# Scores of the unsplit tiles on 64 rows per head, with two PSUM banks of their own

## The chip, the core and the metric

The kernel runs on one core of a Trainium2 chip. The metric is the time of one execution on the device in microseconds (us). A core has a matrix engine (TensorE, PE in the profile, its weight loads shown apart as PEld), VectorE (DVE), ScalarE (ACT), GpSimd (POOL) and SyncE (SP), which here issues nearly all DMAs. Each engine takes its instructions in order; between engines they wait for semaphores. Matmuls write to PSUM, an accumulator memory of eight banks with 512 float32 per partition each; VectorE and ScalarE read it from there.

## What is computed

Attention over 512 local and 32 global positions in 8 batches of 8 heads of width 64, with a band of 32 positions to either side for the local ones, and then an expert layer over all 4608 tokens. Everything is float32. Cut to what matters:

```python
s_l = concat([scale * q_l @ k_g.T, where(|i - j| <= 32, scale * q_l @ k_l.T, -1e9)])
out_l = softmax(s_l) @ concat([v_g, v_l])
out_g = softmax(scale * q_g @ concat([k_g, k_l]).T) @ concat([v_g, v_l])
x = concat([out_g, out_l]) as [4608 tokens, 512]
h = max(x @ w1, x @ w2, x @ w3)
return h @ w_out
```

## The kernel before

**Tiles.** A pair of heads `p` has four tiles of 128 queries (`t` = 0 to 3), 128 tiles in all. A tile sees a window of 192 keys (`t` = 0, 3) or 224 (`t` = 1, 2), since the band reaches no further and the 32 global keys are put among the others. For each tile `scores` (L314) makes one score block per head in PSUM, VectorE adds the mask and takes the row minimum (L342), ScalarE takes the exponential (L344), and the row is normalised. `trans` (L355) transposes the probabilities on TensorE into the tile `T`; a copy `pt` of it feeds `pv` (L391), the product with `v`. `transg`, `glob` and, for the first four pairs, `late` do the same for the global queries. `layer1` (L441) and `layer2` (L462) are the expert layer.

**Split and unsplit tiles.** From tile 28 on, float32 operands are split into two parts that a faster form of the matmul takes (`split_q`, `split_k`, L339). The first 28 tiles (`NATK`) use plain float32 (L335). There the keys of both heads lie in one tile, head 0 on partitions 0 to 63 and head 1 on 64 to 127, and the host sends `q` as 128 x 256: for each head 128 columns with the other head's 64 rows set to zero. So one matmul over all 128 rows gives one head's scores. In the profile such a matmul has two records. `pv` of the first 26 tiles (L401) writes head 0 to output partitions 0 to 63 and head 1 to 64 to 127, on 64 columns of the array each (128*64 in the profile).

**PSUM.** Of the eight banks, three belong to the expert layer (`pm`), two to the pool `psS` (tiles named S, two buffers), one to `T`, and two to the pool `psO` (a tile named O of two banks, one buffer). S is used by `scores`, `glob`, `transg` and `late`; O by `pv` and by the last step of `late` (L519). Accesses of one tile in the same bank are kept in order across engines, whichever columns they touch.

**Order.** A loop over the tiles in the order `SEQ` (L209) puts, for tile i: `transg`, `trans` of tile i + 1, a few layer-1 matmuls of an earlier batch (`fill`), `scores` of tile i + 3, `pv` of tile i, a step of the global queries, loads and, for 24 steps, a piece of the weights, which arrive as float64 and are converted on ScalarE, VectorE and GpSimd (L175 to L181). A scheduler then reorders the instructions of each engine within what the data allow. Tiles 0 to 15 (`EARLY`) come in an order that does half a sequence of four pairs at a time, and their probabilities stay in SBUF (`early`); from tile 16 on they go through a DMA into `prob`, from which they are transposed.

Of the kernel before, what the change touches and what calls it, by code (L numbers as in the profile page):

```python
# [9 lines left out]
F32 = mybir.dt.float32  # L10
# [8 lines left out]
B, H, SL, SG, D = 8, 8, 512, 32, 64  # L19
DM, DF = 512, 768  # L20
NP = H // 2
# [4 lines left out]
NATK = range(0, 28)  # L26
# [24 lines left out]
def f32(ap):  # L51
    return ap.bitcast(F32)


def body(ctx, tc, kin, qin, vin, min_, win, out):
    nc = tc.nc
    act, dve, pool, pe = nc.scalar, nc.vector, nc.gpsimd, nc.tensor

    const = ctx.enter_context(tc.tile_pool(name="const", bufs=1))
    att = ctx.enter_context(tc.tile_pool(name="att", bufs=2))  # L60
# [3 lines left out]
    psS = ctx.enter_context(tc.tile_pool(name="psS", bufs=2, space=PSUM))  # L64
    psT = ctx.enter_context(tc.tile_pool(name="psT", bufs=1, space=PSUM))
    psO = ctx.enter_context(tc.tile_pool(name="psO", bufs=1, space=PSUM))
# [15 lines left out]
    def spend(es, ns):  # L82
        for e in es:
            load[e] += ns
# [69 lines left out]
    turned = psT.tile([128, 512], F32, name="T")  # L154
    dve.memset(turned, 0.0)

    spare = [moe.tile([128, 2, 512], I32, name="spare", tag=f"h{f}") for f in (4, 5)]
    loaded, marks = [0], {}

# [47 lines left out]
    NAT = 26  # L207
    EARLY = 16
    SEQ = [4 * p + t for h in range(2) for p in range(NP) for t in (2 * h, 2 * h + 1)] + list(range(16, NS))  # L209
    kraw, kst, qraw, qs, vraw, vs, xr, sc, pg, pts = [{} for _ in range(10)]  # L210
# [32 lines left out]
    def load_q(s):  # L243
        if s < NS:
            if s in NATK:
                e = s < EARLY and SEQ.index(s) % 2
                qraw[s] = att.tile([128, 256], F32, name="qn", tag="qraw" if e else "qs")
            else:
                qraw[s] = att.tile([128, 256], F32, name="qraw")
            nc.sync.dma_start(out=qraw[s], in_=qin[s])  # L250

    def split_q(s):
        if s < NS and s not in NATK:
# [60 lines left out]
    def scores(sl):  # L314
        if sl >= NS:
            return
        p, t = divmod(sl, 4)
        c0, n = WIN[t]
        ps = psS.tile([128, 512], F32, name="S")
        if sl < EARLY:  # L320
            s = sc[sl] = early[:, SEQ.index(sl) % 4]
        else:
            s = att.tile([128, 2, 224], F32, name="s")
            sc[sl] = prob[sl % 2]
        nm = small.tile([128, 2], F32, name="nm")
        z = small.tile([128, 2], F32, name="z")
        ph = [ps[:, 0:224], ps[:, 224:448]]
        if sl < EARLY:
            keys, c0 = khalf[p][0], c0 - khalf[p][1]
        elif sl in NATK:  # L330
            keys = kraw[p]
        for j in range(2):
            if sl in NATK:

                pe.matmul(ph[j][:, 0:n], lhsT=qraw[sl][:, 128 * j:128 * j + 128], rhs=keys[:, c0:c0 + n],  # L335
                          start=True, stop=True)
                continue
            for a in range(2):
                pe.matmul(ph[j][:, 0:n], lhsT=qs[sl][:, a, 128 * j:128 * j + 128],  # L339
                          rhs=kst[p][:, j, c0:c0 + n], start=(a == 0), stop=(a == 1))  # L340
        for j in range(2):
            dve.tensor_tensor_reduce(out=s[:, j, 0:n], in0=ph[j][:, 0:n], in1=mask[:, (1, 0, 1, 0)[t], 32 * (t == 0):32 * (t == 0) + n],  # L342
                                     scale=-0.125, scalar=3.0e38, op0=ALU.add, op1=ALU.min, accum_out=nm[:, j:j + 1])
            act.activation(out=s[:, j, 0:n], in_=s[:, j, 0:n], func=AF.Exp, bias=nm[:, j:j + 1], scale=-1.0,  # L344
                           accum_out=z[:, j:j + 1])
        for j in range(2):
            dve.tensor_scalar(out=z[:, j:j + 1], in0=z[:, j:j + 1], scalar1=1e-9, scalar2=None, op0=ALU.add)  # L347
            dve.reciprocal(out=z[:, j:j + 1], in_=z[:, j:j + 1])
            times(s[:, j, 0:n], s[:, j, 0:n], z[:, j:j + 1])
        if sl >= EARLY:  # L350
            nc.sync.dma_start(out=f32(sc[sl])[:, :, 0:n], in_=s[:, :, 0:n])
        spend("d", 2 * (n * 1.04 + 75) + 150)
        spend("a", 2 * (n * 0.833 + 278))
# [37 lines left out]
    def pv(sl):  # L391
        p, t = divmod(sl, 4)
        pt = pts.pop(sl)
        o = psO.tile([128, 2, 512], F32, name="O")
        if t == 0:
            xr[p] = xp.tile([128, 4, 160], F32, name="xr")
        if sl < NAT:

            for c, j in ((0, 0), (0, 1), (1, 0), (1, 1)):
                n = 160 if sl >= EARLY and c < GCH[t][2] else 128  # L400
                pe.matmul(o[64 * j:64 * j + 64, 0, 0:n], lhsT=vraw[sl][:, 2 * j + c], rhs=pt[:, j, c, 0:n], start=(c == 0), stop=(c == 1))  # L401
            n = 160 if sl >= EARLY else 128
            copy(xr[p][:, t, 0:n], o[:, 0, 0:n], True)
        else:

            for j in range(2):
                for c in range(2):
                    n = 160 if c < GCH[t][2] else 128
                    pe.matmul(o[:, j, 0:320].rearrange("p (a q) -> p a q", a=2)[:, :, 0:n],  # L409
                              lhsT=vs[sl][:, 2 * j + c].rearrange("p a d -> p (a d)"),  # L410
                              rhs=pt[:, j, c, :, 0:n], start=(c == 0), stop=(c == 1))
            lo = att.tile([64, 2, 160], F32, name="lox", bufs=1)
            copy(lo, o[64:128, :, 0:160], True)
            spend("d", 460 + 2 * 320)
            dve.tensor_tensor(out=lo, in0=o[0:64, :, 160:320], in1=lo, op=ALU.add)
            for j in range(2):
                dve.tensor_tensor(out=xr[p][64 * j:64 * j + 64, t], in0=o[0:64, j, 0:160], in1=lo[:, j], op=ALU.add)  # L417
        if t == 3 and sl >= EARLY:
            dve.tensor_reduce(out=xg[:, p % NP, p // NP], in_=xr[p][:, :, 128:160].rearrange("p t g -> p g t"),
                              axis=AX.X, op=ALU.add)  # L420
# [75 lines left out]
    def late(p):  # L496
        k, v = side[:, 0:640], side[:, 640:1664].rearrange("p (t x) -> p t x", t=4)
        nc.sync.dma_start(out=k, in_=kin[p])
        nc.sync.dma_start(out=v, in_=vin[4 * p:4 * p + 4].rearrange("t p x -> p t x"))
        yield  # L500
        s, nm, z = side[0:64, 0:NG], small.tile([64, 2], F32, name="nmg"), small.tile([64, 2], F32, name="zg")
        for i, (c0, n) in enumerate(SEG):
            ps = psS.tile([128, 512], F32, name="S")
            pe.matmul(ps[0:64, 0:n], lhsT=k[:, KW:KW + 2 * SG], rhs=k[:, c0:c0 + n], start=True, stop=True)
            dve.tensor_tensor_reduce(out=s[:, 384 * i:384 * i + n], in0=ps[0:64, 0:n], in1=zero[0:64].to_broadcast([64, n]),
                                     scale=-0.125, scalar=3.0e38, op0=ALU.add, op1=ALU.min, accum_out=nm[:, i:i + 1])
            spend("d", n * 1.04 + 75)
        yield
        soft(s, nm, z)
        yield  # L510
        g = psS.tile([128, 512], F32, name="S")
        for x, (t, c, c0) in enumerate(PARTS):
            pe.transpose(g[:, 64 * x:64 * x + 64], side[0:64, c0:c0 + 128], one[0:64, 0:64])
        gt = att.tile([128, 6, 64], F32, name="gt", tag="lox", bufs=1)
        dve.tensor_tensor(out=gt, in0=g[:, 0:384].rearrange("p (x g) -> p x g", g=64), in1=cover.to_broadcast([128, 6, 64]), op=ALU.mult)
        o = psO.tile([128, 2, 512], F32, name="O")
        for x, (t, c, _) in enumerate(PARTS):
            for j in range(2):
                pe.matmul(o[64 * j:64 * j + 64, 0, 0:SG], lhsT=v[:, t, 64 * (2 * j + c):64 * (2 * j + c) + 64],  # L519
                          rhs=gt[:, x, SG * j:SG * j + SG], start=(x == 0), stop=(x == 5))  # L520
        copy(xg[:, p, 0], o[:, 0, 0:SG], True)
        yield
# [44 lines left out]
    for i, sl in enumerate(SEQ):  # L567
# [52 lines left out]
        elif i % 16 >= 12:  # L620
            q = b * NP + i % 16 - 12
# [9 lines left out]
def _pack(q_l, k_l, v_l, q_g, k_g, v_g):  # L631
# [8 lines left out]
    g = np.concatenate([ga, gb], axis=3).transpose(0, 1, 3, 4, 2, 5).reshape(B, NP, 128, 2 * SG)  # L640
    k = np.ascontiguousarray(np.concatenate([k, g], axis=3)).reshape(B * NP, 128, KW + 2 * SG)
    q = q_l.reshape(B, NP, 2, 4, 128, D).transpose(0, 1, 3, 5, 2, 4).reshape(B * NP * 4, D, 256)
    q2 = q.reshape(B * NP * 4, D, 2, 128)
    z = np.zeros_like(q2[:, :, 0])
    qz = np.concatenate([np.concatenate([q2[:, :, 0], z], axis=2), np.concatenate([z, q2[:, :, 1]], axis=2)], axis=1)
    q = np.concatenate([q, q], axis=1)
    q[NATK.start:NATK.stop] = qz[NATK.start:NATK.stop]
    vt = [v_l[:, :, 32 * u:32 * u + 32] for u in range(16)] + [v_g]
    zero = np.zeros_like(v_g)
    v = np.concatenate([x for r in VROWS for x in [vt[u] for u in r] + [zero] * (4 - len(r))], axis=2)  # L650
# [1 line left out]
    q, v = np.ascontiguousarray(q), np.ascontiguousarray(v)  # L652
# [34 lines left out]
```

## Time and profile before

| | us |
|---|---|
| runs of before: median of three | 828.65 |
| runs of before: lowest, highest | 827.93, 828.94 |
| the profiled execution's own time | 830.49 |
| its span, first to last instruction | 828.7 |
| TensorE busy | 803.0 |
| VectorE busy | 614.8 |
| ScalarE busy | 510.2 |
| GpSimd busy | 459.3 |

Busy times are those of the profiled execution and overlap one another. A row of the timeline gives the start in us from the span's start, the duration in us, the engine, the line of the kernel, the operation, the tile written and those read, the part of the array that a matmul uses (rows*columns), the shape and the number of records put together; in brackets stands how long the engine had been idle and what ended that. Starts of matmuls are measured and their ends are modelled, so times between starts are used.

### The profile page before, as it was taken

Reading aid. Unit: us, or ns where it says so; the run is one execution under the profiler, and the core shown is the slowest. Engines: PE = TensorE matmul, PEld = TensorE weight load, DVE = VectorE, ACT = ScalarE, POOL = GpSimd, SP = SyncE. Lnnn points to the kernel's source line nnn. Section 1 sums busy time; section 2 is a strip of 40 time slices with the busy share of each in tenths; the row PEclk is TensorE's granted clock in tenths of the full one; section 3 lists DMA queues with packets and bytes.
Section 4 is the critical chain, followed back from the end, with each engine's and each line's share of the span. In section 5 each row is a group of like instructions: output and inputs, shape, how many; then the busy total and the mean of one; then the engine's idle time right before and its main releaser. Section 6 shows DMA issues by size and latency. Waiting matters only on the chain.

```text
span 828.7 us, 16580 instructions
## 1 busy us (share of the span) xinstructions
PE 803.0 (97%) x4772; PEld 683.8 (83%) x4772; DVE 614.8 (74%) x2192; ACT 510.2 (62%) x1416; POOL 459.3 (55%) x623
## 2 busy tenths in 40 slices
PE   6788999999999999999999999999999999999997
PEld 5577888888888888888888888888888888888896
DVE  6999997878887888888887888788887888412111
ACT  5888786666666666666766667676666666311111
POOL 3223355756676667767675676866776665311211
PEclk9989999999999999999999999999999999999999
DMA  8956555533335333443335333443335332100001
GB/s 295 314 178 224 169 152 149 165 116 99 116 108 152 112 97 104 131 136 94 99 104 170 112 98 97 127 139 98 97 96 165 110 100 63 60 13 1 25 27 26
DMA packets 97466, 98.15 MB, mean 118 GB/s; under 512 B 19296, under 2 KB 85856, under 8 KB 97376
## 3 DMA queue, kind: packets, MB, share of 16 engines
q1 hardware_dynamic: 97232, 96.87, 38.0%
q8 instruction: 38, 0.62, 0.3%
q14 instruction: 52, 0.43, 0.2%
q10 hardware_dynamic: 144, 0.23, 0.1%
HBM read 60.39 MB, written 8.91 MB: 84 GB/s over the span
## 4 chain that ended last, share of the span: by engine, by line
PE 80%; DVE 5%; DMA 4%; issue 3%; ACT 3%; POOL 3%; SPq 1%; POOLq 0%; ACTq 0%; DVEq 0%
PE pm L441 45%; PE pm L462 16%; PE O L409 6%; PE S L339 5%; PE T L362 2%; PE T L363 2%; DMA prob<-s 2%; PE S L289 1%; PE S L335 1%; POOL h L103 1%; PE O L401 1%; DMA vraw<-v_in 1%; ACT s L344 1%; PE S L381 1%; DMA raw<-w_in 1%
## 5 line engine op out<-in xcount | busy, mean ns | idle before, releaser
L441 PE MATMUL pm<-xs,w 128*128 128x512 f32 (+1 forms) x2160 | 487.3, 366 | 1.3 <-ACT m L115 0.9
L441 PEld LDWEIGHTS pm<-xs,w 128*128 128x128 f32 x2160 | 354.3, 190 | 52.7 <-issue 4.2
L462 PE MATMUL pm<-w,h 128*128 128x512 f32 x612 | 157.5, 397 | 2.3 <-POOL h L103 2.1
L103 POOL TENSOR_TENSOR h<-m,h 128x512 fp32r<-128x512 f32 (+1 forms) x59 | 70.3, 1192 | 108.5 <-ACT h L115 107.9
L462 PEld LDWEIGHTS pm<-w,h 128*128 128x128 f32 x612 | 109.0, 188 | 23.0 <-POOL h L103 4.4
L450 DVE TENSOR_TENSOR m<-pm,m 128x512 f32<-128x512 f32 (+1 forms) x120 | 72.8, 607 | 66.3 <-PE pm L441 65.6
L103 POOL TENSOR_TENSOR qs<-qraw,qs 128x256 fp32r<-128x256 f32 x100 | 76.7, 767 | 70.4 <-issue 34.8
L344 ACT ACTIVATE s<-s,nm 128x192 f32<-128x192 f32 (+1 forms) x224 | 103.3, 462 | 19.6 <-DVE nm L342 14.1
L125 POOL TENSOR_SCALAR s<-s,z 128x224 f32<-128x224 f32 (+1 forms) x192 | 83.9, 444 | 36.1 <-ACT lox L115 20.4
L342 DVE CUSTOM_DVE_ANT_0 s<-S,mask 128x192 f32<-128x192 f32 (+1 forms) x224 | 74.5, 369 | 15.2 <-PE S L339 7.0
L103 DVE TENSOR_TENSOR pt<-T,pt 128x512 fp32r<-128x512 f32 x102 | 70.4, 690 | 19.4 <-ACT pt L115 18.2
L103 POOL TENSOR_TENSOR vs<-vraw,vs 128x256 fp32r<-128x256 f32 x102 | 75.6, 741 | 12.6 <-ACT vs L115 9.3
L409 PEld LDWEIGHTS O<-pt,vs 128*128 128x128 f32 x408 | 66.2, 188 | 9.9 <-issue 1.6
L409 PE MATMUL O<-pt,vs 128*128 128x320 f32 (+1 forms) x408 | 72.9, 300 | 1.4 <-DVE pt L103 1.4
L339 PEld LDWEIGHTS S<-kst,qs 128*128 128x128 f32 x400 | 59.5, 190 | 8.7 <-DVE nmg L293 0.2
L417 DVE TENSOR_TENSOR xr<-O,lox 64x160 f32<-64x160 f32 x204 | 64.4, 315 | 3.1
L103 POOL TENSOR_TENSOR kst<-kraw,kst 64x576 fp32r<-64x576 f32 x44 | 63.9, 1453 | 4.3 <-DMA prob<-s 1.0
L115 ACT CAST pt<-T 128x512 fp32r<-128x512 f32 x102 | 60.3, 591 | 9.5 <-PE T L363 7.1
L115 ACT CAST qs<-qraw 128x256 fp32r<-128x256 f32 x94 | 38.3, 407 | 44.0 <-PE S L339 28.8
L115 ACT CAST h<-m 128x512 fp32r<-128x512 f32 (+1 forms) x59 | 33.2, 562 | 51.7 <-DVE m L450 51.6
L339 PE MATMUL S<-kst,qs 128*128 128x192 f32 (+1 forms) x400 | 59.5, 270 | 0.0
L347 DVE TENSOR_SCALAR z<-z 128x1 f32<-128x1 f32 x256 | 37.5, 147 | 27.1 <-ACT s L344 17.9
(123 smaller groups left out, 1183.7 us busy)
## 6 DMA issues: line engine op xcount, KB each, us to landing
vraw<-v_in SPq DMA_DIRECT2D x122, 128.0 KB, 2.3
qraw<-q_in SPq DMA_DIRECT2D x100, 128.0 KB, 2.2
prob<-s SPq DMA_DIRECT2D x56, 224.0 KB, 2.5
raw<-w_in SPq DMA_DIRECT2D x24, 512.0 KB, 5.3
prob<-s SPq DMA_DIRECT2D x56, 192.0 KB, 2.3
out_dram<-o SPq DMA_DIRECT2D x32, 256.0 KB, 2.4
kraw<-k_in SPq DMA_DIRECT2D x25, 320.0 KB, 3.1
qn<-q_in SPq DMA_DIRECT2D x29, 128.0 KB, 3.6
```

Source lines behind the costliest of these rows:

```text
L103: (dve if least(c) == "d" else pool).tensor_tensor(out=out, in0=a, in1=b, op=ALU.subtract)
L115: act.copy(out=out, in_=a)
L125: pool.tensor_scalar(out=out, in0=a, scalar1=col, scalar2=1.0, op0=ALU.mult, op1=ALU.mult)
L339: pe.matmul(ph[j][:, 0:n], lhsT=qs[sl][:, a, 128 * j:128 * j + 128], rhs=kst[p][:, j, c0:c0 + n], start=(a == 0), stop=(a == 1))
L342: dve.tensor_tensor_reduce(out=s[:, j, 0:n], in0=ph[j][:, 0:n], in1=mask[:, (1, 0, 1, 0)[t], 32 * (t == 0):32 * (t == 0) + n], scale=-0.12 ...
L344: act.activation(out=s[:, j, 0:n], in_=s[:, j, 0:n], func=AF.Exp, bias=nm[:, j:j + 1], scale=-1.0, accum_out=z[:, j:j + 1])
L347: dve.tensor_scalar(out=z[:, j:j + 1], in0=z[:, j:j + 1], scalar1=1e-9, scalar2=None, op0=ALU.add)
L409: pe.matmul(o[:, j, 0:320].rearrange("p (a q) -> p a q", a=2)[:, :, 0:n], lhsT=vs[sl][:, 2 * j + c].rearrange("p a d -> p (a d)"), rhs=pt[ ...
L417: dve.tensor_tensor(out=xr[p][64 * j:64 * j + 64, t], in0=o[0:64, j, 0:160], in1=lo[:, j], op=ALU.add)
L441: pe.matmul(ps[:, 0:n], lhsT=weight(3 * f + i, w)[:, 128 * k:128 * k + 128], rhs=xs[k][:, a, c0:c0 + n], start=(q == 0), stop=(q == 11))
L450: dve.tensor_tensor(out=m[:, 0:n], in0=ps[:, 0:n], in1=m[:, 0:n], op=ALU.max)
L462: pe.matmul(ps, lhsT=hh[f][:, a, 128 * t:128 * t + 128], rhs=weight(18 + f, w), start=(q == 0), stop=(q == 17))
```

## The change

Three edits, for the 28 unsplit tiles.

The host packs `q` as 128 x 128: head 0 on partitions 0 to 63, head 1 on 64 to 127, with no zeros. The load is 64 KB instead of 128 KB.

The score matmul of head j takes rows 64j to 64j + 63 of `q` and of the keys, so the two heads of a tile use different rows of the array and write to different banks.

The tile that was the single O buffer is taken once at the start (`both`) and holds the scores of all 28 tiles, head 0 in the first bank and head 1 in the second, even places of the order in columns 0 to 223 and odd ones in 224 to 447. `pv` of the first 26 tiles and the last step of `late` use an S buffer instead. From tile 26 on `pv` has O again, and from tile 28 on `scores` has S again.

```diff
+    both = psO.tile([128, 2, 512], F32, name="O")
...
-                qraw[s] = att.tile([128, 256], F32, name="qn", tag="qraw" if e else "qs")
+                qraw[s] = att.tile([128, 128], F32, name="qn", tag="qraw" if e else "qs")
+                nc.sync.dma_start(out=qraw[s], in_=qin[s, :, 0:128])
...
-        ps = psS.tile([128, 512], F32, name="S")
+        if sl in NATK:
+            c = 224 * (SEQ.index(sl) % 2)
+            ph = [both[:, j, c:c + 224] for j in range(2)]
+        else:
+            ps = psS.tile([128, 512], F32, name="S")
+            ph = [ps[:, 0:224], ps[:, 224:448]]
...
-                pe.matmul(ph[j][:, 0:n], lhsT=qraw[sl][:, 128 * j:128 * j + 128], rhs=keys[:, c0:c0 + n],
+                pe.matmul(ph[j][:, 0:n], lhsT=qraw[sl][64 * j:64 * j + 64], rhs=keys[64 * j:64 * j + 64, c0:c0 + n],
                           start=True, stop=True)
...
-        o = psO.tile([128, 2, 512], F32, name="O")
+        o = psO.tile([128, 2, 512], F32, name="O") if sl >= NAT else psS.tile([128, 1, 512], F32, name="S")
...
-        o = psO.tile([128, 2, 512], F32, name="O")
+        o = psS.tile([128, 1, 512], F32, name="S")
...
-    q2 = q.reshape(B * NP * 4, D, 2, 128)
-    z = np.zeros_like(q2[:, :, 0])
-    qz = np.concatenate([np.concatenate([q2[:, :, 0], z], axis=2), np.concatenate([z, q2[:, :, 1]], axis=2)], axis=1)
+    qn = np.concatenate([q[:, :, 0:128], q[:, :, 128:256]], axis=1)
     q = np.concatenate([q, q], axis=1)
-    q[NATK.start:NATK.stop] = qz[NATK.start:NATK.stop]
+    q[NATK.start:NATK.stop, :, 0:128] = qn[NATK.start:NATK.stop]
```

The change moves instructions, because the scheduler sees other waits. Every engine has the same instructions as before, apart from the size of the q loads, and from the first matmuls of layer 2 on TensorE's order is the same. In the new kernel L335 is L341, L362 and L363 are L368 and L369, L381 is L387, L401 is L407, L441 is L447, L285 is L287, L504 is L510, L342 is L348.

The first matmuls of the program on TensorE, with the semaphores they wait for (DMAHW: a load; DVE: VectorE). Before:

```order
L335 MATMUL S<-kh,qn 128x192 [waits DMAHW2_49,DMAHW1_49]
L335 MATMUL S<-kh,qn 128x192
L335 MATMUL S<-kh,qn 128x224 [waits DMAHW3_49]
L335 MATMUL S<-kh,qn 128x224
L335 MATMUL S<-kh,qn 128x192 [waits DMAHW6_49,DMAHW4_49,DVE_49]
L335 MATMUL S<-kh,qn 128x192
L335 MATMUL S<-kh,qn 128x224 [waits DMAHW7_49,DVE_49]
L335 MATMUL S<-kh,qn 128x224
L362 MATMUL T<-one,early 128x128 [waits DVE_49,Pool_49]
```

And now:

```order
L341 MATMUL O<-kh,qn 128x192 [waits DMAHW2_49,DMAHW1_49]
L341 MATMUL O<-kh,qn 128x192
L341 MATMUL O<-kh,qn 128x224 [waits DMAHW3_49,DVE_49]
L341 MATMUL O<-kh,qn 128x224
L341 MATMUL O<-kh,qn 128x192 [waits DMAHW6_49,DMAHW4_49,DVE_49]
L341 MATMUL O<-kh,qn 128x192
L368 MATMUL T<-one,early 128x128 [waits DVE_49,Pool_49]
```

The second tile's scores now wait for VectorE too, that is for its reads of the first tile in the same banks, and tile 3's scores have moved behind the first transposes. This wait of each tile for the tile before it holds on through tile 27. On VectorE, tile 3's reads move likewise behind two steps of the weights' conversion.

Tiles 6 and 7 on TensorE (tiles are numbered by their place in `SEQ`). Before:

```order
L335 MATMUL S<-kh,qn 128x192 x2
L401 MATMUL O<-pt,vn 64x128
L362 MATMUL T<-one,early 128x128
L363 MATMUL T<-one,early 64x128
L401 MATMUL O<-pt,vn 64x128
L362 MATMUL T<-one,early 128x128
L363 MATMUL T<-one,early 64x128
L401 MATMUL O<-pt,vn 64x128 x2
L441 MATMUL pm<-xs,w_308 128x256 x2
L335 MATMUL S<-kh,qn 128x224 x2
```

And now:

```order
L341 MATMUL O<-kh,qn 128x192 x2
L447 MATMUL pm<-xs,w_303 128x256 x3
L368 MATMUL T<-one,early 128x128
L369 MATMUL T<-one,early 96x128
L407 MATMUL S<-pt,vn 64x128 x3
L368 MATMUL T<-one,early 128x128
L369 MATMUL T<-one,early 96x128
L407 MATMUL S<-pt,vn 64x128
L447 MATMUL pm<-xs,w_303 128x256
L447 MATMUL pm<-xs,w_343 128x256 x2
L341 MATMUL O<-kh,qn 128x224 x2
```

Both pieces run from the scores of tile 6 to those of tile 7. Between them stood `pv` of tile 3 and two layer-1 matmuls, and now stand `pv` of tile 4 and six: the scores have moved back by about a tile.

Tile 19, just behind the transposes of tile 17 (the `prob` rows). Before:

```order
L362 MATMUL T<-identr,prob_94 128x128
L363 MATMUL T<-identr,prob_94 96x128
L441 MATMUL pm<-xs,w_1078 128x256 x9
L381 MATMUL S<-identr,probg_95 128x128
L335 MATMUL S<-kn,qn 128x192 x2
L401 MATMUL O<-pt,vraw 64x160 x2
L401 MATMUL O<-pt,vraw 64x128 x2
L285 MATMUL S<-kn 64x384
L441 MATMUL pm<-xs,w_1145 128x256 x10
L381 MATMUL S<-identr,probg_95 128x128
```

And now:

```order
L368 MATMUL T<-identr,prob_94 128x128
L369 MATMUL T<-identr,prob_94 96x128
L447 MATMUL pm<-xs,w_1061 128x256 x4
L341 MATMUL O<-kn,qn 128x192 x2
L447 MATMUL pm<-xs,w_1061 128x256 x4
L387 MATMUL S<-identr,probg_95 128x128
L447 MATMUL pm<-xs,w_1061 128x256
L447 MATMUL pm<-xs,w_1127 128x256
L407 MATMUL S<-pt,vraw 64x160 x2
L407 MATMUL S<-pt,vraw 64x128 x2
L287 MATMUL S<-kn 64x384
L387 MATMUL S<-identr,probg_95 128x128
```

The scores of tile 19 stood next to `pv`; now they stand between layer-1 matmuls. The second L387, which takes the S buffer that `pv` had, follows `pv` and the global scores at once instead of ten layer-1 matmuls later.

More of the change, by code (lines that the diff above doesn't have):

```diff
@@ L246, in load_q @@
                 e = s < EARLY and SEQ.index(s) % 2
-                qraw[s] = att.tile([128, 256], F32, name="qn", tag="qraw" if e else "qs")
+                qraw[s] = att.tile([128, 128], F32, name="qn", tag="qraw" if e else "qs")
+                nc.sync.dma_start(out=qraw[s], in_=qin[s, :, 0:128])
             else:
                 qraw[s] = att.tile([128, 256], F32, name="qraw")
-            nc.sync.dma_start(out=qraw[s], in_=qin[s])
+                nc.sync.dma_start(out=qraw[s], in_=qin[s])
     def split_q(s):
@@ L326, in scores @@
         z = small.tile([128, 2], F32, name="z")
-        ph = [ps[:, 0:224], ps[:, 224:448]]
         if sl < EARLY:
```

## Prediction

> **What bounds the kernel now.** I read first the page's shares, then the busy time by stretches, since a share of 97% hides stages. Columns: stretch in us, its length, busy us (x count) of TensorE (PE), weight loads (PEld), VectorE (DVE), ScalarE (ACT) and GpSimd (POOL), granted clock, DMA share, GB/s.
>
> ```profile
> span 828.7 us, 16580 instructions
> PE 803.0 (97%) x4772; PEld 683.8 (83%) x4772; DVE 614.8 (74%) x2192; ACT 510.2 (62%) x1416; POOL 459.3 (55%) x623
> ...
> 20.00:80.00 60.00, 53.34 (x382) 43.34 (x380) 58.07 (x193) 51.23 (x143) 17.13 (x16) 0.94 0.73 247
> 80.00:130.00 50.00, 47.46 (x397) 40.37 (x397) 43.50 (x161) 37.61 (x116) 18.88 (x18) 0.97 0.51 153
> ...
> 152.00:828.00 676.00, 669.25 (x3742) 571.68 (x3741) 481.74 (x1701) 395.90 (x1085) 401.29 (x547) 1.00 0.33 98
> ```
>
> From 152 us on TensorE works without a break that matters, and its order there is the same in both kernels. So the change can only move the moment at which that stretch begins. From 20 to 80 us it is VectorE that is full (58.07 of 60); TensorE has 6.7 us to spare. From 80 to 130 us TensorE leads (47.46 of 50) and VectorE has 6.5 us to spare. Next the timeline of TensorE, for two rows that waited (start, duration, what; in brackets the idle time and what ended it):
>
> ```profile
> 82.67 0.28 PE L362 MATMUL T<-identr,prob 128*128 128x128 f32 x1 [1.18 <-DMA prob<-s]
> ...
> 145.49 0.82 PE L409 MATMUL O<-pt,vs 128*128 128x320 f32 x4 [1.37 <-DVE pt L103]
> ```
>
> The row at 82.67 is the transposing of tile 17 (it waits for a DMA that moves `prob`, behind softmax work on the full VectorE). Before it, cheaper matmuls only make TensorE wait longer. After it, until the last changed tile (27, at 128 us), what TensorE saves or loses counts nearly one for one. Up to this row both kernels put the same 183 layer-1 matmuls, so the two sides of it can be priced apart.
>
> **The change part by part.** *Half the contraction rows, two heads at once.* A float32 matmul shows as two records. This stretch of the timeline gives all prices:
>
> ```profile
> 13.95 0.92 PE L335 MATMUL S<-kh,qn 128*128 128x192 f32 x4
> 14.71 0.27 PE L362 MATMUL T<-one,early 128*128 128x128 f32 x1
> ...
> 14.92 0.27 PE L362 MATMUL T<-one,early 128*128 128x128 f32 x1
> 15.03 0.27 PE L363 MATMUL T<-one,early 128*64 128x128 f32 x1
> 15.24 0.66 PE L401 MATMUL O<-pt,vraw 128*64 128x128 f32 x8
> 15.82 1.02 PE L335 MATMUL S<-kh,qn 128*128 128x224 f32 x4
> 16.68 0.27 PE L362 MATMUL T<-one,early 128*128 128x128 f32 x1
> ```
>
> Four score records take 0.76 us at 192 columns (13.95 to 14.71) and 0.86 at 224; the difference, 0.10 over 4 x 32 columns, is 0.8 ns a column, so a record is 0.16 or 0.19 us. The `pv` matmuls (L401) already run two heads side by side, on 64 columns of the array each: eight records of 128 columns last 0.58 us (15.24 to 15.82), where transposes as wide cost 0.11 each and eight would cost 0.88. Side by side, then, a pair costs one record. No row of this profile shows a pair split by rows: its saving lies between nothing and half of the four records. I take half, by the nearest row, `pv`: 0.32 us for a 192 tile, 0.38 for a 224 tile. The Trainium skill, page "TensorE: Matmul & The Clock Gate", Part 3, gives a measured 3.07 times for four row tiles of 32 rows; scaled to two, an estimate of 1.5 times, the same tiles would save a third instead of half, and the sum would be 0.9 us worse; no run shown here decides it.
>
> *Which tiles count.* Behind tile 17's transposes come the scores of tiles 19 to 27:
>
> ```profile
> L335 PEld LDWEIGHTS S<-kn,qn x36: 186/190/337, 84.8 to 128.3; 128*128 128x128 f32 x36
> L335 PE MATMUL S<-kn,qn x36: 323/352/628, 84.9 to 128.5; 128*128 128x192 f32 x20, 128*128 128x224 f32 x16
> ...
>   DVE s L342: 4.1, 2
> ```
>
> That is five tiles of 192 and four of 224. In the new order tile 24 has its two heads apart, with `pv` and transposes between, so it gains no overlap: 4 x 0.32 + 4 x 0.38 = **2.8 us saved**. VectorE waited 4.1 us for these scores, which says again that TensorE leads here.
>
> *Changing how the array is split.* The same rows show that going to the split array and back isn't free. From the last transpose (15.03) to `pv` are 0.21 us, 0.10 over a transpose's step. `pv` itself has 0.58 for four pairs of 0.11, 0.14 over. The next scores take 0.86 instead of 4 x 0.19, 0.10 over. One trip there and back costs 0.34, 0.17 a change. The one group that uses 64 rows today, L513, costs the same:
>
> ```profile
> 130.43 1.37 PE L441 MATMUL pm<-xs,w 128*128 128x256 f32 x10
> 131.63 0.22 PE L381 MATMUL S<-identr,probg 128*128 128x128 f32 x1
> ...
> 146.25 0.58 PE L513 MATMUL S<-one,side 64*128 64x64 f32 x6
> 146.76 1.46 PE L441 MATMUL pm<-xs,w 128*128 128x256 f32 x10
> 148.05 0.23 PE L381 MATMUL S<-identr,probg 128*128 128x128 f32 x1
> ```
>
> Ten layer-1 matmuls last 1.20 us in a row (130.43 to 131.63) and 1.29 behind L513; six L513 records of 64 columns, at 0.8 ns a column 0.31, last 0.51. Before, scores ran on the whole array like the layer-1 matmuls and transposes beside them. Now each tile between two of those pays a trip, and one beside `pv` half a trip. Counted in the two orders from tile 17's transposes to those of tile 28, the array changes 32 times before and 51 times now: 19 x 0.17 = **3.2 us lost**. The Trainium skill, page "TensorEngine Tiling (Array Packing)", Tiling Modes, Key Properties, says that changing the tiling mode drains the engine; it names no price. By that rule the trips are paid in full as above, and the trace agrees with its 0.34 us; if they were free, the sum would be 3.2 us better (a rival below).
>
> *The two banks held for scores.* Each score pair now waits until VectorE has read the tile before it, whatever its columns. In the early tiles that read is late:
>
> ```profile
> 20.82 0.92 PE L335 MATMUL S<-kh,qn 128*128 128x224 f32 x4
> ...
> 23.58 0.08 DVE L342 DVE_READ_ACCUMULATOR2_ANT nm<- 128x1 f32 x1
> ...
> 23.87 0.43 PE L401 MATMUL O<-pt,vn 128*64 128x128 f32 x2
> ...
> 89.46 0.81 PE L335 MATMUL S<-kn,qn 128*128 128x192 f32 x4
> ...
> 91.84 0.35 DVE L342 CUSTOM_DVE_ANT_0 s<-S,mask 128x192 f32<-128x192 f32 x1
> ...
> 95.11 0.98 PE L335 MATMUL S<-kn,qn 128*128 128x224 f32 x4
> ```
>
> Tile 7's scores began at 20.82, tile 6's were read until 23.66. Queued behind such a wait on TensorE are `pv`, transposes and layer 1, and the ScalarE copies of these wait in turn. But the new order puts tile 7's scores behind `pv` 4, whose last records started at 23.87, after that read; and this is where VectorE leads. Behind tile 17 the longest lag is tile 20's, 1.6 us from the end of its scores (90.27) to its first read, and tile 21's scores start only at 95.11. I take 0, bounds 0 and 2.5 us.
>
> *`pv` in the S pool.* It shares two slots with the global scores, whose reader may be slow. Nearest rows, waits for a slot's reader and for `pv` by its copy:
>
> ```profile
> PE S L289 <- DVE nmg L505: 0.5, 1, 0.5
> ...
> ACT xr L115 <- PE O L401: 2.5, 2, 1.4
> ```
>
> A slot wait cost 0.5 us once; ScalarE stood ready for `pv`, so its copy comes promptly. The order has four places where a slot's next user follows `pv` or the global scores closely: 0 to 2.0 us, and I take **0.4 lost**. On the other side the wait of `pv` for its single old buffer goes, in the stretch that VectorE sets: nothing.
>
> *Half the q bytes.* Four loads of 128 KB stand ahead of the first weight piece, on which ScalarE waits; 262 KB less at 292 GB/s is 0.9 us.
>
> ```profile
> qn<-q_in SPq DMA_DIRECT2D x29, 128.0 KB, 3.6
> ...
> 0.00:20.00 20.00, 12.79 (x76) 10.01 (x76) 12.13 (x62) 10.65 (x33) 7.25 (x24) 1.00 0.89 292
> ...
> 40.00:60.00 20.00, 17.42 (x120) 15.51 (x121) 18.77 (x61) 17.37 (x47) 6.12 (x5) 0.83 0.53 183
> ...
> 10.13 0.38 DVE L342 CUSTOM_DVE_ANT_0 early<-S,mask 128x224 f32<-128x224 f32 x1
> ...
> 10.51 0.38 DVE L342 CUSTOM_DVE_ANT_0 early<-S,mask 128x224 f32<-128x224 f32 x1
> ...
> 10.65 0.67 ACT L175 ACTIVATE spare<-raw 128x512 f32<-128x512 f32 x1 [1.52 <-DMA raw<-w_in]
> ...
> 11.79 0.15 DVE L347 TENSOR_SCALAR z<-z 128x1 f32<-128x1 f32 x1 [0.65 <-ACT early L344]
> 12.22 0.15 DVE L347 TENSOR_SCALAR z<-z 128x1 f32<-128x1 f32 x1 [0.28 <-ACT early L344]
> ```
>
> VectorE's waits (0.93 us) come from that. But tile 3's reads (two steps of 0.3 us from 10.13 on), which stood ahead of these waits, stand behind them now. 0.9 - 0.6 = **0.3 saved**; bounds 0 and 0.9. Later q loads land well before use.
>
> **Sum.** -0.3 - 2.8 + 3.2 + 0.4 = +0.5 us on the profiled execution's own 830.49 (span 828.7 and 1.8 around it): 831.0. The three runs shown have a median of 828.65; the same +0.5 gives 829.15, say 829.1.
>
> **The rivals.**
> *Changes of the array hide.* Weight loads for the idle half could start early. For it: loads overlap in every steady stretch. Against it: the 0.34 us in the rows above, and L513. Without 3.2: -2.7, that is 825.9. Chance 0.16.
> *The row pair doesn't overlap (slower).* The four records run one behind the other, 2.8 comes back: +3.3, 832.0. It decides where TensorE leads, tiles 19 to 27; it needs the pair's records to start a full record apart rather than together. For it: no row shows such a pair, and a 128-column weight load takes 190 ns (the row of tiles 19 to 27). Against it: `pv`. Chance 0.18.
> *Waits for reads take over (slower).* Score pairs or slots wait for VectorE at tiles 16 to 27, 2 us in all more than I took: 831.1. Against it: reads within 1 us there. Chance 0.14.
> *Nothing arrives.* The wait of 1.37 us at 145.49 swallows what TensorE loses, since the chain that ends it runs through loads of `v` (below), ScalarE and VectorE: 828.4. Chance 0.10.
>
> ```profile
> 129.43 4.23 DMA vraw<-v_in
> ```
>
> The forecast has 0.42, with 827.6 to 830.2 as its own range.
>
> **How the numbers follow.** A measurement of this kernel can tell about 0.2%, 1.7 us, from no change. Faster by more: the first rival (0.16) and a little of the others, 0.18. Slower: the second and third (0.32, less their lower edges) and the forecast's upper edge, 0.32. Same: 0.50. The range reaches from the first rival to the second with the bounds of the slot waits: 825.9 to 832.4.
>
> **What would show it.** Right: score records in pairs that start a few ns apart; a first layer-1 step near 0.2 us behind them; tile 17's transposes 0.3 us earlier, with TensorE idle longer before them; tile 27's scores within 1 us of 128. Wrong: score records 0.16 us apart one by one; layer-1 steps of 0.12 right behind scores; new rows in which scores or `pv` wait for VectorE by over 0.5 us after 83 us; a lower granted clock in 50 to 130 us, since an idler TensorE showed 0.83 in 40 to 60 us.

## The result, and the profile after

| | before | after |
|---|---|---|
| median of the runs taken side by side, us | 828.8 | 835.42 |
| lowest to highest | 827.93 to 829.13 | 835.09 to 836.89 |
| the profiled execution's own time / span | 830.49 / 828.7 | 836.89 / 835.1 |
| first layer-2 matmul | 152.28 | 158.92 |
| tile 11's first transpose | 49.69 | 54.47 |
| TensorE busy over the span | 803.0 | 808.4 |

After is **slower by 0.72%** (ratio 1.0072, 95% interval 1.0046 to 1.0097), 6.0 us by the ratio and 6.6 by the medians where 0.5 us was forecast, and outside the range. From the first layer-2 matmul to the end both need the same time (676.4 and 676.2 us), so all of it is lost ahead of that matmul.

Where? The next two fences are busy times by stretches, before and then after, cut at tile 11's first transpose (columns as in the prediction).

```profile
0.00:49.69 49.69, 36.31 (x223) 27.57 (x224) 41.47 (x159) 36.65 (x103) 15.14 (x30) 0.93 0.77 256
49.69:152.28 102.59, 97.67 (x812) 84.87 (x811) 91.89 (x336) 77.92 (x230) 43.16 (x47) 0.98 0.60 189
```

```profile
0.00:54.47 54.47, 40.53 (x218) 25.57 (x219) 42.43 (x159) 36.55 (x103) 15.44 (x30) 0.85 0.69 229
54.47:158.92 104.45, 98.70 (x816) 80.23 (x816) 92.72 (x336) 77.73 (x230) 43.15 (x48) 0.98 0.54 170
```

The second stretch is TensorE's: busy 97.67 of 102.59 us, with nearly the same matmuls in both kernels (812 and 816 records). Of the 6.64 us, 4.78 are lost by tile 11 and 1.86 behind it. That is a count by one marker: at tile 17's transposes after is 2.48 us late, since between these two markers TensorE waited 2.5 us before (0.4, 0.9 and 1.2) and 0.5 us after. Part of the early loss is made up there, and the other 4.16 us are lost behind tile 17. The first stretch shows two things: VectorE does the same work (41.47 and 42.43 us) in a longer time, and the granted clock is 0.85 instead of 0.93.

TensorE's waits in the first 160 us of after (us in total, times, the longest) name a first cause:

```profile
PE T L368 <- ACT early L123: 3.4, 3, 2.2
PE O L341 <- DVE nm L348: 3.1, 3, 1.5
PE S L387 <- DVE xr L113: 1.9, 1, 1.9
PE O L415 <- DVE pt L103: 1.4, 1, 1.4
```

Before, scores waited once for a read of VectorE (1.4 us in all). Now they wait three times; the timeline of after shows the first two (line, operation, rows*columns of the array; the idle time in brackets):

```profile
4.23 1.01 PE L341 MATMUL O<-kh,qn 64*128 64x192 f32 x4 [4.23 <-DMA qn<-q_in]
5.97 1.12 PE L341 MATMUL O<-kh,qn 64*128 64x224 f32 x4 [0.74 <-DVE nm L348]
7.90 1.01 PE L341 MATMUL O<-kh,qn 64*128 64x192 f32 x4 [0.81 <-DVE nm L348]
...
10.27 1.12 PE L341 MATMUL O<-kh,qn 64*128 64x224 f32 x4
```

Four tiles' scores stood in one run of sixteen records before (4.51 to 9.28). Now each pair stands behind VectorE's read of the tile ahead of it: tile 3's begin at 10.27 instead of 8.44, and in the first 20 us VectorE is busy 11.06 instead of 12.13 us. Tile 7's begin at 27.02 instead of 20.82, and from 20 to 40 us VectorE is busy 17.18 instead of 19.65 us, but there TensorE's clock is low as well (below). In a second profile of after, where the clock is full until 36 us, VectorE is busy 19.94 us from 20 to 40.

The wait of 1.9 us is the third one of the list. TensorE's timeline of after, and then VectorE's:

```profile
111.49 0.71 PE L407 MATMUL S<-pt,vraw 128*64 128x160 f32 x8
112.03 0.81 PE L287 MATMUL S<-kn 128*64 128x384 f32 x2
114.74 0.28 PE L387 MATMUL S<-identr,probg 128*128 128x128 f32 x1 [1.90 <-DVE xr L113]
```

```profile
111.05 1.87 DVE L103 TENSOR_TENSOR kst<-kraw,kst 64x576 fp32r<-64x576 f32 x1
112.95 1.38 DVE L178 TENSOR_SCALAR wct<-wct 128x512 int32<-128x512 int32 x1
114.25 0.20 DVE L353 TENSOR_SCALAR z<-z 128x1 f32<-128x1 f32 x2
114.38 0.31 DVE L113 COPY xr<-S 128x160 f32<-128x160 f32 x1
```

`pv` of tile 20 and the global scores hold both S slots; the transpose L387 needs the first, and its copy `xr` stands on VectorE behind two long operations. Before, `pv` was in O and this wait did not exist.

The third thing is the clock. The page's windows of after show it from 20 to 60 us:

```profile
20.00:40.00 20.00, 17.27 (x97) 11.09 (x97) 17.18 (x58) 13.62 (x40) 5.97 (x5) 0.74 0.53 166
40.00:60.00 20.00, 15.59 (x102) 11.88 (x102) 18.96 (x62) 17.86 (x50) 5.06 (x4) 0.83 0.63 207
```

Summed over windows of 2 us, TensorE ran at half its clock for 17.0 us of the first 56; before, for 6.8. (The first 20 us read 1.00 in this column; more on that in the last section.)

### The profile page after: what moved, and what is told of

The parts are those of the page before. It is cut to its first block, busy times and chain, and to the rows that moved or that the text cites. A ratio compares the mean times of both kernels' runs of the same rounds, so it can differ in the third digit from the quotient of the medians.

```text
span 835.1 us, 16588 instructions
## 1 busy us (share of the span) xinstructions
PE 808.4 (97%) x4772; PEld 677.1 (81%) x4772; DVE 618.7 (74%) x2192; ACT 510.9 (61%) x1416; POOL 459.7 (55%) x623
## 4 chain that ended last, share of the span: by engine, by line
PE 82%; DVE 6%; issue 3%; DMA 3%; POOL 3%; ACT 2%; SPq 1%; POOLq 0%; DVEq 0%; ACTq 0%
PE pm L447 47%; PE pm L468 15%; PE O L415 6%; PE S L345 5%; DMA prob<-s 2%; PE T L368 2%; PE T L369 2%; PE S L291 1%; PE S L407 1%; POOL h L103 1%; PE S L387 1%; PE O L341 1%; DVE s L348 1%; DMA raw<-w_in 1%; ACT s L350 1%
## 5 line engine op out<-in xcount | busy, mean ns | idle before, releaser
L447 PE MATMUL pm<-xs,w 128*128 128x512 f32 (+1 forms) x2160 | 489.0, 367 | 0.9 <-POOL w L103 0.9
L447 PEld LDWEIGHTS pm<-xs,w 128*128 128x128 f32 x2160 | 354.9, 190 | 55.9 <-issue 8.3
L350 ACT ACTIVATE s<-s,nm 128x192 f32<-128x192 f32 (+1 forms) x224 | 103.9, 465 | 20.6 <-DVE nm L348 15.7
L348 DVE CUSTOM_DVE_ANT_0 s<-S,mask 128x192 f32<-128x192 f32 (+1 forms) x200 | 66.6, 370 | 10.6 <-PE S L345 5.8
```

Source lines behind the costliest of these rows:

```text
L447: pe.matmul(ps[:, 0:n], lhsT=weight(3 * f + i, w)[:, 128 * k:128 * k + 128], rhs=xs[k][:, a, c0:c0 + n], start=(q == 0), stop=(q == 11))
```

## The experiments

All times are medians, with the ratio to the kernel before on the same chip and its interval. T11 is tile 11's first transpose and L2 the first layer-2 matmul, both of the profiled execution. The profile of the rows without banks is of its slowest run (844.13), that of after with no hold in tiles 0 to 7 of its fastest (832.23).

| run | us | ratio (95%) | T11 | T11 to L2 | half clock in the first 56 us |
|---|---|---|---|---|---|
| before | 828.7 to 830.1 | | 49.69 | 102.6 | 6.8 |
| after, first runs | 835.42 | 1.0072 (1.0046 to 1.0097) | 54.47 | 104.5 | 17.0 |
| after, again | 836.22 | 1.0068 (1.0042 to 1.0095) | 53.85 | 104.8 | 17.0 |
| banks without rows | 836.24 | 1.0070 (1.0044 to 1.0095) | 52.15 | 106.3 | 6.8 |
| rows without banks | 838.73 | 1.0112 (1.0071 to 1.0153) | 57.23 | 108.4 | 6.2 |
| tiles 0 to 15 alone | 835.22 | 1.0054 (1.0035 to 1.0074) | 55.62 | 102.5 | 20.5 |
| tiles 16 to 27 alone | 832.42 | 1.0017 (1.0000 to 1.0035) | 48.73 | 104.4 | 6.8 |
| after, three S buffers | 837.13 | 1.0089 (1.0057 to 1.0122) | 55.07 | 104.7 | 20.4 |
| before, three S buffers | 832.18 | 1.0032 (1.0014 to 1.0049) | 48.77 | 105.0 | 3.4 |
| after, 96 idle matmuls | 847.16 | 1.0201 (1.0170 to 1.0232) | 62.54 | 105.8 | 0.2 |
| before, 96 idle matmuls | 842.33 | 1.0142 (1.0105 to 1.0179) | 59.16 | 105.6 | 0 |
| after, 18 idle matmuls | 834.63 | 1.0055 (1.0035 to 1.0076) | 52.44 | 103.8 | 6.8 |
| after, no hold in tiles 0 to 7 | 836.26 | 1.0083 (1.0055 to 1.0111) | 51.04 | 102.8 | 6.8 |
| the same, 18 idle matmuls | 834.40 | 1.0072 (1.0055 to 1.0089) | 50.53 | 103.9 | 10.3 |
| banks without rows, no hold in tiles 0 to 7 | 830.87 | 1.0031 (1.0016 to 1.0047) | 49.16 | 103.3 | 10.2 |
| tiles 16 to 27, half the hold | 834.69 | 1.0054 (1.0035 to 1.0074) | 50.86 | 106.0 | 10.3 |

**The two parts of the change, each alone.** First the banks without the rows; TensorE's instructions stand in the same order as after.

```diff
-                pe.matmul(ph[j][:, 0:n], lhsT=qraw[sl][64 * j:64 * j + 64], rhs=keys[64 * j:64 * j + 64, c0:c0 + n],
+                pe.matmul(ph[j][:, 0:n], lhsT=qraw[sl][:, 128 * j:128 * j + 128], rhs=keys[:, c0:c0 + n],
```

> The banks without the rows: scores of the 28 unsplit tiles are held in the two O banks and the products with v go to S, as in the change, but a score matmul again takes 128 rows with zeros, and q has its 128 KB. TensorE's order is that of the changed kernel. Theory 1 (the loss is the wait of the scores for VectorE's read of the tile before, and the S slots): the loss stays, 834 to 838 us. Theory 2 (the loss is the changing of the array's split, with what the halved clock adds to it): it goes, 828 to 830 us. In between: both have a part, and the difference to the changed kernel is the part of the rows.

It kept the whole loss (836.24). So the banks are enough for it by themselves, and with the banks held the rows change the sum by nothing that can be measured. That the rows cost nothing alone does not follow (see the hold taken away, below).

```diff
-            c = 224 * (SEQ.index(sl) % 2)
-            ph = [both[:, j, c:c + 224] for j in range(2)]
+            ph = [psS.tile([128, 512], F32, name="S")[:, 0:224] for _ in range(2)]
```

> The rows without the banks: a score matmul takes 64 rows per head and q comes with 64 KB, but each head's scores go to an S buffer of their own, and the products with v keep O. Theory 1: scores may run ahead again, 828 to 831 us (a tile now takes both S slots, which may cost one or two us by itself). Theory 2: the array's split is changed as often as in the changed kernel, 833 to 837 us.

838.73: worse than after, and no answer to the question put. A tile takes both S slots here, so its scores again wait for the reads of the tile ahead (three waits, 1.5 us), and many pairs came apart.

**The two halves of the tiles.** The edit is a condition on the tile's number in `scores`, `load_q` and `pv`.

```diff
-        if sl in NATK:
+        if sl < EARLY:
             c = 224 * (SEQ.index(sl) % 2)
```

> The change for tiles 0 to 15 alone: from tile 16 on scores take 128 rows and an S buffer, and v's products and the late step take O from the thirteenth place on. If the start makes the loss (scores one tile at a time, TensorE at half clock until 17 us and again from 24 to 34 us), the first layer-2 matmul is 4 to 6 us late and the time 833 to 835 us. If the S slots at tiles 20 to 24 make it, 829 to 831 us.

> The change for tiles 16 to 27 alone: before that scores take 128 rows and an S buffer, and v's products O. If the start makes the loss, 828 to 830 us; if the S slots at tiles 20 to 24 make it (v's products, the global scores and the transposes of the global queries in two slots), 832 to 835 us.

The early half alone loses 5.9 us by T11 and nothing behind it (102.5 us from T11 to L2, as before). The later half alone loses 1.8 us between T11 and L2 and gains 1.0 ahead of it; its time, at a ratio of 1.0017 with an interval from 1.0000, can hardly be told from no change. The early half costs by far the more. The wait of 1.9 us at L387 does not stand in the later half's trace, so what makes its 1.8 us is not shown.

**More S buffers.**

```diff
-    pm = ctx.enter_context(tc.tile_pool(name="pm", bufs=3, space=PSUM))
-    psS = ctx.enter_context(tc.tile_pool(name="psS", bufs=2, space=PSUM))
+    pm = ctx.enter_context(tc.tile_pool(name="pm", bufs=2, space=PSUM))
+    psS = ctx.enter_context(tc.tile_pool(name="psS", bufs=3, space=PSUM))
```

> The changed kernel with three S buffers and two pm buffers instead of two and three. If the S slots that v's products share with the global scores and transposes make the loss between tiles 20 and 24, the wait of 1.9 us at 114.7 us goes, tile 24's two heads stand together, tile 24's transposes are at most 3 us behind those of its control (the kernel before with the same buffers) instead of 6.3, and the time is 3 to 4 us nearer to that control. If the held score banks make it, the distance to the control stays at 6 us or more.

> The control: the kernel before with three S buffers and two pm buffers. One pm buffer less can make layer 1 wait for its readers: 829 to 836 us, whatever the theory. A third S buffer has little to give here, since only 0.5 us of TensorE's waits stood for a slot.

The wait of 1.9 us went (one of 1.4 us for the same copy, at the global scores, came), and the distance to the control stayed at 5.0 us. In the profiles after is 6.3 us behind its control at T11, and from there to L2 it takes no longer (104.7 and 105.0 us). The slots do not make the early loss.

**The clock.** Matmuls that nothing reads keep TensorE busy.

```diff
+    def warm(n):
+        ps = pm.tile([128, 512], F32, name="pm")
+        for _ in range(n):
+            pe.matmul(ps[:, 0:128], lhsT=one, rhs=one, start=True, stop=True)
...
+        if i < 8:
+            warm(10)
         fill(3)
```

> The changed kernel with matmuls that nothing reads (identity by identity into a pm buffer): 16 ahead of the first tile's transposes and 10 behind v's product of each of the first eight tiles. If the halved clock (until 17 us and from 24 to 34 us) makes the early loss, it goes, tile 9's transposes are back at 39 to 40 us instead of 42.9 and the time falls by 1 to 3 us. If the held banks make it, tile 9 stays at 42 us or later and the time at 835 us or above.

> The control: the kernel before with the same matmuls that nothing reads. Before, only the stretch from 42 to 49 us had the halved clock among the first 80 us, so little can be won: 828 to 831 us by either theory.

They held the clock up but cost 11 to 13 us in both kernels. The expectations had their price wrong: such a matmul is two records, not one. In the control:

```profile
19.57 2.50 PE L552 MATMUL pm<-one 128*128 128x128 f32 x20
21.90 0.27 PE L362 MATMUL T<-one,early 128*128 128x128 f32 x1
```

Twenty records, ten matmuls, take 2.33 us, and all 96 matmuls some 22 us. Of these, 9.5 us arrived at T11; TensorE's idle time ahead of T11 fell from 13.4 to 7.0 us, and the half clock went. So **extra work of TensorE in the early tiles fills idle time first, and what is left arrives**, though VectorE is 97% busy there. With hardly any half clock in either kernel the distance between the two is still 4.8 us instead of 6.6, and 3.4 instead of 4.8 at T11. A smaller dose, ahead of the transposes:

```diff
+        if 2 <= i < 8:
+            warm(3)
         trans(tile_at(i + 1))
```

> The changed kernel with only three matmuls that nothing reads ahead of each of the transposes of tiles 3 to 8 (18 in all, 0.11 us each at full clock, so at most 2 us on the chain, less where TensorE waited anyway). If the halved clock costs the early part 2 us or more, the half-clock stretch from 24 to 34 us goes and tile 11's transposes come at 52 to 54 us. If it costs nothing, tile 11 comes at 55 to 56.5 us.

> The changed kernel itself beside the others on one chip, for comparison: 834 to 837 us by every theory; its first layer-2 matmul 5 to 7 us behind that of the kernel before, tile 11's transposes 3 to 5 us, the more of it the longer the half clock before tile 11 lasts.

The half clock fell from 17.0 to 6.8 us and T11 came 1.4 to 2.0 us earlier than in the two runs of after, although some 4 us of idle matmuls (36 records of 0.11 us) stood on TensorE; the time fell by 1.6 us by the medians, which the intervals do not tell from nothing. The two profiles of after have the same 17.0 us of half clock, in other places: tile 8's transposes are 4.6 us late in one and 1.2 in the other, T11 4.8 and 4.2.

**The hold taken away** in the first eight places, with 64 rows, and then with full rows:

```diff
+            i = SEQ.index(sl)
+            if i % 2 and i < 8:
+                ph = [pm.tile([128, 512], F32, name="pm")[:, 0:224] for _ in range(2)]
+            else:
+                ph = [both[:, j, 224 * (i % 2):224 * (i % 2) + 224] for j in range(2)]
```

> The changed kernel, but the scores of tiles at odd places among the first eight go to two pm buffers instead of the held banks (layer 1, which uses pm, has hardly begun by then), so that the first four tiles' scores run one behind the other and no early score waits for the tile before it. If the hold makes the early loss, tile 11's transposes are at 50 to 52 us instead of 54.5 and the time is 2 to 3 us below the changed kernel's. If the halved clock makes it by itself (fewer rows, idler TensorE), tile 11 stays at 53 us or later unless the stretch from 24 to 34 us at half clock goes too, which this run shows beside it.

> The changed kernel with both early remedies: odd tiles among the first eight in two pm buffers, and three matmuls that nothing reads ahead of the transposes of tiles 3 to 8 (0.11 us each, at most 2 us). If hold and halved clock are all of the early loss, tile 11's transposes come at 50 to 52 us, with the clock of the runs at 0.993 or above, and the time is 831 to 834 us, what is left being the matmuls themselves and the later part. If something else holds the early tiles, tile 11 stays at 53 us or later.

> The banks without the rows (128 rows with zeros, 128 KB of q), and the scores of odd tiles among the first eight in two pm buffers. With the hold in all early tiles this form had tile 11's transposes at 52.15 us, 2.5 us behind the kernel before. If that was the hold, they come at 49.7 to 51 us and the time falls by 1 to 3 us, to 832 to 835 us; if it was the S slots of v's products, they stay at 52 us and the time at 836 us.

With full rows this is nearly the kernel before: 830.87 us, T11 at 49.16, 3.0 us earlier than with the hold. The difference arises at the start: VectorE's work in the first 20 us, first with the hold and then without, differs by those 3.0 us (10.26 and 13.26), while from 20 to 40 us it is about full in both (19.94 and 19.44).

```profile
0.00:20.00 20.00, 13.50 (x64) 9.67 (x64) 10.26 (x54) 9.76 (x28) 5.83 (x22) 1.00 0.85 278
```

```profile
0.00:20.00 20.00, 14.31 (x84) 11.51 (x84) 13.26 (x62) 11.63 (x36) 8.15 (x24) 1.00 0.92 311
```

The first scores without the hold, and the stretch from T11 to L2:

```profile
4.51 1.62 PE L344 MATMUL O<-kh,qn 128*128 128x192 f32 x4 [4.51 <-DMA qn<-q_in]
5.92 1.70 PE L344 MATMUL pm<-kh,qn 128*128 128x224 f32 x4
7.41 1.49 PE L344 MATMUL O<-kh,qn 128*128 128x192 f32 x4
8.69 1.32 PE L344 MATMUL pm<-kh,qn 128*128 128x224 f32 x4
...
49.16:152.45 103.29, 97.83 (x816) 84.69 (x816) 91.49 (x335) 77.68 (x229) 42.89 (x48) 0.99 0.58 179
```

No wait stands between these scores. The stretch behind T11 is 3.0 us shorter too: the wait for the S slot, 2.0 us in the run with the hold, isn't there, although `pv` is still in S, with the instructions around that transpose now in another order. The clock in this stretch is also higher, 0.99 for 0.96, so how much of the 3.0 us is the wait stays open.

With 64 rows T11 came to 51.04, as expected of the hold, but the time did not follow: 836.26 us, from 832.23 (clock 0.995 over the run) to 838.35. Its profiled run is the 832.23. With the idle matmuls 834.40, of which up to 4 us may be those matmuls. So without the early hold 64 rows are slower than full rows by 0.52% (1.0083 and 1.0031), some 4.3 us; with it, they are equal (1.0068 to 1.0072 and 1.0070). **Either part of the change is enough alone, the held banks with full rows or 64 rows without the early hold, and only without both is more than half of the loss gone.**

**Where the lag arises.** Each tile's first transpose against that of the kernel before, in us, one profile each:

| run | tile 1 | 5 | 6 | 8 | 9 | 11 | 17 | half clock in the first 56 us |
|---|---|---|---|---|---|---|---|---|
| after, first profile | -0.97 | 1.09 | 4.50 | 4.64 | 4.52 | 4.78 | 2.48 | 24 to 34, from 48 |
| after, again | -0.36 | 1.04 | 2.23 | 1.18 | 3.84 | 4.16 | 1.37 | 36 to 53 |
| after, no hold in tiles 0 to 7 | -0.58 | 1.19 | 1.19 | 1.19 | 1.41 | 1.35 | -2.46 | 44 to 51 |
| banks without rows | 1.26 | 1.94 | 3.11 | 2.06 | 2.17 | 2.46 | 1.44 | 46 to 53 |
| banks without rows, no hold in tiles 0 to 7 | -1.19 | -1.19 | -1.09 | -1.08 | -0.88 | -0.53 | -3.12 | 40 to 50 |

(Before has its own half clock from 42 to 49 us.) In after 1.0 to 1.1 us are there by tile 5, and without the hold 1.2: with 64 rows, taking the hold away gains nothing by then. The rest of after's lag comes in steps where TensorE runs at half clock: 3.4 us between tiles 5 and 6 in one profile, 2.7 between tiles 8 and 9 in the other. With full rows the hold's lag is there from tile 1 on.

**The later half with half the hold:** head 0 in an S slot, head 1 in the second bank of O, `pv` in its first.

```diff
-            ph = [both[:, j, c:c + 224] for j in range(2)]
+            ph = [psS.tile([128, 512], F32, name="S")[:, 0:224], both[:, 1, 0:224]]
```

> The change for tiles 16 to 27 alone and with half the hold: 64 rows per head, head 0 in an S buffer as before, head 1 in the second bank of O, and v's products in the first bank of O, none in S. Tiles 0 to 15 as before. If the S slots shared with v's products and the double hold make the later loss (3.7 us from tile 11 to layer 2 with full rows) and the rows by themselves gain 1 to 2 us there, 827 to 829 us, at or a little under the kernel before. If the changing of the array's split takes the gain, 830 to 832 us.

834.69, by neither reason. The heads of tiles 16 to 23 wait for different things and stand apart in TensorE's queue. Its timeline, for a tile whose heads follow one another but did not start together:

```profile
95.89 0.64 PE L343 MATMUL S<-kn,qn 64*128 64x224 f32 x2
96.35 0.64 PE L343 MATMUL O<-kn,qn 64*128 64x224 f32 x2
96.93 1.58 PE L453 MATMUL pm<-xs,w 128*128 128x256 f32 x11
...
50.86:156.82 105.96, 101.88 (x812) 83.73 (x811) 90.76 (x336) 78.65 (x231) 43.05 (x47) 0.98 0.56 175
```

One head costs 0.46 to 0.58 us, nearly what the pair costs (0.58, below). TensorE is busy 101.88 us behind T11 instead of 97.67: eight tiles at some 0.5 us.

## Why the prediction was wrong, step by step

**The pair's overlap and the price of the array's split: right where they can be read alone.** The same four groups of rows, a layer-1 run, a 224 tile's scores, five layer-1 matmuls and `pv`, first before and then after:

```profile
116.01 0.94 PE L441 MATMUL pm<-xs,w 128*128 128x256 f32 x6
116.79 0.92 PE L335 MATMUL S<-kn,qn 128*128 128x224 f32 x4
117.38 0.91 PE L441 MATMUL pm<-xs,w 128*128 128x256 f32 x5
118.22 0.71 PE L401 MATMUL O<-pt,vraw 128*64 128x160 f32 x8
```

```profile
122.26 0.94 PE L447 MATMUL pm<-xs,w 128*128 128x256 f32 x6
123.13 0.65 PE L341 MATMUL O<-kn,qn 64*128 64x224 f32 x4
123.71 0.86 PE L447 MATMUL pm<-xs,w 128*128 128x256 f32 x5
124.50 0.71 PE L407 MATMUL S<-pt,vraw 128*64 128x160 f32 x8
```

From the first row to the last: 2.21 us before, 2.24 after. The two heads' records start 7 ns apart, so the second rival (no overlap) falls. From the scores to `pv` the new rows are 0.06 us quicker (1.37 for 1.43), and the layer-1 run ahead of them is 0.09 slower (0.87 for 0.78), which is where leaving the whole array would show. If two of the four records are saved, 0.38 us as the prediction had it, the way to the split array and back costs 0.41 where it had 0.34; the two cancel. The first rival (changes of the split hide) falls with it.

**"Before it, cheaper matmuls only make TensorE wait longer": the step that failed.** From this, and from "this is where VectorE leads", the prediction counted nothing ahead of tile 17 but the 0.3 us of the q loads. The waits there did swallow part of what was lost: 4.78 us at tile 11 are 2.48 at tile 17, and 4.16 are 1.37 in the other profile. They did not swallow all, and the early half alone, with the change in no tile behind, is 5.8 us late at the first layer-2 matmul. VectorE leads in that stretch only as long as scores lie ready for it and TensorE keeps its clock.

**The two held banks: 0 us taken, bounds 0 and 2.5; the term that was most clearly mis-sized.** The prediction looked at two tiles, 7 and 21, found the read done by the time the new order asks, and took that for all. It did not look at the first four tiles, whose scores ran ahead before. With full rows, taking the hold out of the first eight tiles brings T11 3.0 us forward, more than the upper bound, and the time from 836.24 to 830.87 us, ratios 1.0070 and 1.0031: some 3.2 us by the ratios, whose intervals just touch (1.0044 and 1.0047). With 64 rows the same step did not bring the time back, so the hold is not the whole cause of the loss as it was made.

**Behind tile 17: 0.8 us lost (-2.8, 3.2 and 0.4) was forecast, 4.16 measured.** From tile 17's first transpose to the first layer-2 matmul, first before and then after:

```profile
82.67:152.28 69.61, 67.23 (x574) 58.67 (x575) 60.60 (x233) 50.87 (x152) 33.37 (x37) 0.98 0.54 160
85.15:158.92 73.77, 68.70 (x575) 55.32 (x575) 63.98 (x239) 51.59 (x155) 33.75 (x39) 0.98 0.48 147
```

TensorE is idle 5.07 us instead of 2.38 and busy 68.70 instead of 67.23 for as many records. Of the idle time 1.9 us are the S slot. Of the 1.5 us of busy time the array's terms had 0.4; the rest stays open.

**The clock: named as a sign, not priced.** The prediction named a lower clock from 50 to 130 us as a sign of being wrong; that stretch reads 0.95 for 0.98 before, but most of the half clock came ahead of it, from 24 to 34 us (and from 36 to 53 in the other profile). How much of the loss it makes can only be estimated. Ten runs of the kernel with tiles 0 to 15 changed, the same program each time, have spans of 829.4 to 830.5 us at a mean clock of 0.993 to 0.994 (three runs), and of 833.4 to 834.1 at 0.986 to 0.988 (five); the other two are 832.1 at 0.991 and 835.2 at 0.990. A straight line through the ten gives 0.6 us for each 0.001. After has 0.0047 less than the kernel before on average (0.9895 over four runs, 0.9942 over 53), which by that slope would be 2.8 us. At a mean clock of 0.991 or 0.992 after took 835.1 us on average (five runs) and before 831.7 (nine): 3.4 us are left. So by both estimates about half of the loss goes with the clock. The four kernels with 64-row pairs in tiles 0 to 15 and no idle matmuls (after, with three S buffers, without the early hold, and the early half) have mean clocks of 0.987 to 0.990, all others 0.992 or more. This is a correlation: whether the shorter work lowers the clock, and the clock makes the loss, is not shown. The runs without the early hold scatter more (834.9 us at 0.993, 834.0 at 0.984). How much of the 64 rows' 4.3 us there is clock stays open.

**`pv` in the S pool: 0.4 taken, bounds 0 and 2.0; 1.9 measured**, as one wait, in both profiles of after and in that of the banks without the rows (1.9, 1.9, 2.0). It depends on the order around it: it vanished where only the early tiles' buffers were altered, and in the later half alone.

**The q bytes: 0.3 taken.** The first scores start at 4.23 us in one profile of after and at 4.45 in the other, against 4.51; nothing of it reaches the end.

**The rivals.** The third (waits for reads and slots, 2 us in tiles 16 to 27) came about as priced: behind tile 17 TensorE is idle 2.7 us more. That is less than half of the loss, and the start, where score pairs wait as well, was not in it. The fourth (nothing arrives) falls: the wait of 1.4 us for `pt` is there in both kernels and swallowed nothing. Of the signs, the pairs came as forecast; tile 17's transposes came 2.5 us later instead of 0.3 earlier, and tile 27's scores at 133.82 instead of within 1 us of 128.

No kernel tried beats the kernel before. The nearest are the later half alone, 0.17% above it and hardly to be told from it, and full rows without the early hold, 0.31% above.

## What to carry to other kernels

A busy share of 97% on one engine does not say that the others are free: look at the chain of a tile and ask what feeds the full engine. Where results of several tiles are made ahead of their reader, the number of buffers sets how far ahead, and giving two banks to one tile takes that away first at the start, where nothing else is there to do. Before pricing a delay at nothing, count the slack behind it: here some 2 us of waits swallowed part, and the rest arrived. And undoing one part of a change shows only that part's cost beside the other: here each was enough for the whole loss.

## What the runs showed of the hardware

- Two float32 matmuls on 64 rows each, in different banks, start 7 ns apart; going to such a split and back to the whole array cost some 0.4 us around a tile of 224 columns, all that the overlap saved.
- The granted clock in the windows reads 1.00 over the first 20 us of after, but transposes follow each other by 0.21 us until 17.2 us and by 0.11 from then on. Before, with sixteen score records in a row, they are 0.11 apart from 9.28 us on. So at the start a lower speed exists that this column doesn't show, and the half clock of the tables leaves it out.
- TensorE went to half clock in stretches of about 3.4, 6.8, 10.2 and 17 us, in other places from one execution to the next of the same program. With 64-row scores, the early hold and no idle matmuls the first 56 us had 17.0 to 20.5 us of it in four profiles, in all others 0 to 10.3 us. The Trainium skill, page "TensorE: Matmul & The Clock Gate", Part 1, says that the clock is released and taken back by a free-running window of some 3.4 us; the lengths here agree. The abstract rule in the same part, no idle gaps of more than some 3.4 us, was kept here and was not enough: TensorE's longest wait between 5 and 60 us of after was 2.2 us.
